# A hand-ordered attention and GeGLU kernel: the first norm of segments 2 and 3 is applied to x that the host has transposed

## The chip, the core and the metric

The kernel runs on one core of a Trainium2 chip. The metric is the device time of one execution in microseconds, as a median over runs. The engines are called as the profile calls them: PE is TensorE (matmul), DVE is VectorE, ACT is ScalarE, POOL is GpSimd, and SP is SyncE, which here only issues DMAs.

## The reference, cut to what matters

A pre-norm block with 2048 tokens of 512 channels. Its attention has 32 heads of 16 channels and four segments of 512 tokens; within a segment it is a masked softmax, and a memory carries what earlier segments held. A gated feed-forward block of width 1376 follows.

```python
x = A_x
h = x + _A_ref(_layernorm(x, axis=-1), A_wq, A_wk, A_wv, A_wo, A_beta)
h2 = h + _B_ref(_layernorm(h, axis=-1), B_w_gate, B_w_up, B_w_down)
```

The change touches only the first `_layernorm(x)`: for each token, (x - mean) / sqrt(variance + 1e-5) over the 512 channels.

## The kernel before

**Layout.** Rows of x have tokens on the partitions. The projections need the channels there, so each segment's normalized x is wanted transposed, as four tiles `XT[s][dc]` of 128 channels by 512 tokens. Every such tile is held as two parts, hi and lo: hi is the value rounded to the matmul's input type, lo the rest. A product is three matmuls (`SPLIT`: hi hi, hi lo, lo hi).

**The first norm.** `ln1_first` does segment 0 and `ln1(1)` segment 1; both take a square root on ACT and are not touched. `ln1(2)` and `ln1(3)` call `layer_norm` with `off=True`. Its steps for such a segment are: load four row tiles of x (L957); two sums per tile on ACT (L757, L766); small steps on DVE that work out 1/sqrt by Newton's method (`y`, four columns, one for each row tile) and `b = -mean * y` (L830); the scaling `y * x + b` on ACT, row tile by row tile (L834); the transposes on PE with the identity, 64 rows at a time (L847, by the helper `sides`, which also has DVE read one column between its two phases, L574); and `split_psum`, which copies a transposed bank to hi on ACT (L883) and subtracts for lo on DVE (L884).

**Attention.** The work is cut into 16 units of a group of 8 heads and a segment, in the order `UNITS`: segments 0 and 1 for all four groups, then segments 2 and 3. Each unit has two half units of four heads. A unit is projected (`project`, L978, and `vproj`, L1027, on 64-row tiles of PE); DMAs move queries and keys to the score layout (L1104, L1110); `pass_a` takes the score maxima (L1234 on PE, L1244 on DVE, L1258 and L1259 on POOL, L1265, and a store of the maxima into the query tile, L1272); `pass_b` makes scores (L1292), exponentials (L1298, ACT), a mask select on POOL (L1306), and the product with the values (L1320), which works on 32-column tiles of PE, as do the memory update (L1145) and the denominators (L1182).

**Feed-forward.** From about 390 us on, PE does nothing but the output projection and the feed-forward matmuls (L1393, L1584, L1651, L1752).

**The order.** Every instruction is first recorded with its engine and what it reads and writes. `ORDER`, a table of numbers, then says in which order they are issued: each engine works through its own part of that order, waiting on semaphores for what it needs. Buffers come from pools in that order too. The durations written in the code (`dve`, `act`, `pool`, `dma`) serve the search that made the table and decide which buffer is taken; they set no time on the chip. SP issues nearly all DMAs from one queue, also in order, so a DMA that waits holds back those behind it.

## Time and profile before

| what | value |
|---|---|
| median of 3 runs | 734.33 us (734.27 to 734.55) |
| the profiled execution | 732.46 us |
| its span, first to last instruction | 730.7 us |
| instructions | 19228 |
| granted TensorE clock, mean | 0.999 |
| busy: PE, DVE, ACT, POOL | 715.5, 630.8, 535.5, 521.7 us |

The profile is of one execution. A row of a group shows the line, the engine, the operation, what it writes and reads (buffer numbers left out), the count, the busy time in all, the mean of one in nanoseconds, and the idle time of the engine just before with what ended it. A row of the timeline shows the start, the length and the instructions merged into it. Ends of matmuls are modelled and overlap the next work, so starts are the better measure on PE.

### The profile page before, as it was taken

To read this page: it belongs to the slowest core of one execution; us is meant where nothing else is said; L and a number is where in the kernel's file an instruction comes from. 1 tells how busy PE (TensorE), PEld (TensorE's weight loads), DVE (VectorE), ACT (ScalarE), POOL (GpSimd) and SP (SyncE) were. 2 spreads that over 40 slices of the span, in tenths; PEclk is the share of its full clock that TensorE was granted. 3 is DMA by queue.
4 is the path that set the end of the run, shared out by engine and by line. 5 is a ranking of instruction groups with operands and counts; after the bars stand their busy time and mean duration, and the time that the engine had idled before them with its cause. 6 is when DMAs were issued, how large, how long until landed. Compare 5 with 4: busy or idle time off the path is not lost.

```text
span 730.7 us, 19228 instructions
## 1 busy us (share of the span) xinstructions
PE 715.5 (98%) x6436; PEld 573.9 (79%) x6436; DVE 630.8 (86%) x1998; ACT 535.5 (73%) x1139; POOL 521.7 (71%) x815
## 2 busy tenths in 40 slices
PE   6999999999999999999999999999999999999997
PEld 6887878777878887777677878888888878888885
DVE  6897889998979888999987576879999998879996
ACT  6889988797786887967868478678876766656431
POOL 7443434355553664878789999998999977699936
PEclk9999999999999999999999999999999999999999
DMA  7546457456577777687775756677574236876857
GB/s 274 147 119 161 109 125 217 116 133 190 160 182 185 206 201 210 193 232 218 190 229 185 224 159 220 218 204 240 162 201 129 81 105 212 250 241 226 272 132 260
DMA packets 100654, 137.32 MB, mean 188 GB/s; under 512 B 18012, under 2 KB 40460, under 8 KB 100556
## 3 DMA queue, kind: packets, MB, share of 16 engines
q1 hardware_dynamic: 100396, 135.84, 63.8%
q8 instruction: 51, 0.84, 0.5%
q14 instruction: 47, 0.39, 0.2%
q10 hardware_dynamic: 160, 0.26, 0.2%
HBM read 70.67 MB, written 39.26 MB: 150 GB/s over the span
## 4 chain that ended last, share of the span: by engine, by line
PE 89%; DVE 4%; DMA 2%; ACT 2%; POOL 1%; issue 1%; SPq 0%; DVEq 0%; ACTq 0%
PE bank L1584 29%; PE bank L1752 12%; PE bank L978 11%; PE bank L1320 10%; PE bank L1234 6%; PE bank L1292 6%; PE bank L1027 5%; PE bank L1393 3%; PE bank L1651 3%; PE bank L1400 2%; PE bank L1202 1%; POOL row L1306 1%; DVE bank L1244 1%; DMA stk<-slot 1%; DVE aside L1244 1%
## 5 line engine op out<-in xcount | busy, mean ns | idle before, releaser
L1298 ACT ACTIVATE row<-bank 128x512 f32<-128x512 f32 x320 | 171.7, 606 | 34.6 <-PE bank L1292 27.9
L1306 POOL TENSOR_SCALAR_AFFINE_SELECT row<-row 128x128 f32<-128x128 f32 (+1 forms) x320 | 107.1, 363 | 90.4 <-ACT row L1298 88.6
L1244 DVE CUSTOM_DVE_ANT_0 aside<-bank,amask 128x384 f32<-128x384 f32 (+2 forms) x384 | 141.3, 419 | 13.2 <-PE bank L1234 5.1
L978 PE MATMUL bank<-slot,slot 64*128 64x512 f32 x720 | 109.4, 402 | 0.0
L1584 PE MATMUL bank<-slot,slot 128*128 128x512 f32 (+1 forms) x366 | 95.7, 390 | 0.0
L1244 DVE CUSTOM_DVE_ANT_0 bank<-bank,amask 128x512 f32<-128x512 f32 x128 | 86.2, 712 | 9.0 <-PE bank L1234 7.8
L1292 PE MATMUL bank<-stq,stk 64*128 64x128 f32 (+3 forms) x512 | 81.2, 338 | 1.2 <-DVE slot L884 0.7
L1584 PEld LDWEIGHTS bank<-slot,slot 128*128 128x128 f32 (+1 forms) x366 | 67.6, 185 | 15.6
L1320 PE MATMUL bank<-row,vaug 128*32 128x512 f32 (+3 forms) x1024 | 77.1, 436 | 2.0 <-DVE nm L1244 0.8
L978 PEld LDWEIGHTS bank<-slot,slot 64*128 64x128 f32 x720 | 74.0, 185 | 6.4 <-DVE nm L1244 0.5
L1234 PE MATMUL bank<-stk,stq 64*128 64x128 f32 (+3 forms) x512 | 77.1, 327 | 1.2 <-DMA stk<-slot 0.8
L1763 DVE TENSOR_TENSOR row<-row,bank 128x512 f32<-128x512 f32 x110 | 71.9, 676 | 5.3 <-PE bank L1752 3.8
L1292 PEld LDWEIGHTS bank<-stq,stk 64*128 64x128 f32 x512 | 54.6, 185 | 13.9 <-DVE nm L1244 4.3
L1549 POOL TENSOR_TENSOR slot<-row,slot 128x512 fp32r<-128x512 f32 (+3 forms) x57 | 63.7, 1127 | 2.5 <-ACT slot L1547 2.2
L1591 ACT ACTIVATE vaug<-bank 128x512 f32<-128x512 f32 (+1 forms) x66 | 38.9, 595 | 34.4 <-PE bank L1584 33.8
L1234 PEld LDWEIGHTS bank<-stk,stq 64*128 64x128 f32 x512 | 53.4, 185 | 11.5 <-DVE nm L1244 3.0
L1320 PEld LDWEIGHTS bank<-row,vaug 128*32 128x32 f32 x1024 | 31.1, 109 | 38.3 <-issue 31.4
L1752 PE MATMUL bank<-slot,half 128*128 128x512 f32 x234 | 61.2, 389 | 0.0
L1027 PE MATMUL bank<-slot,slot 64*128 64x256 f32 x672 | 51.6, 284 | 0.3 <-DVE bn L763 0.2
L1752 PEld LDWEIGHTS bank<-slot,half 128*128 128x128 f32 x234 | 43.9, 188 | 9.2
L1244 DVE DVE_READ_ACCUMULATOR2_ANT nm<- 128x1 f32 x512 | 49.8, 97 | 0.0
L1027 PEld LDWEIGHTS bank<-slot,slot 64*128 64x128 f32 x672 | 47.4, 186 | 1.1 <-DVE bn L763 0.4
(230 smaller groups left out, 1715.6 us busy)
## 6 DMA issues: line engine op xcount, KB each, us to landing
stq<-slot SPq DMA_DIRECT2D x96, 128.0 KB
stk<-slot SPq DMA_DIRECT2D x94, 128.0 KB
row<-x SPq DMA_DIRECT2D x32, 256.0 KB
pv_dram<-row SPq DMA_DIRECT2D x32, 256.0 KB
row<-r_dram SPq DMA_DIRECT2D x28, 256.0 KB
wd_dram<-half SPq DMA_DIRECT2D x28, 256.0 KB
half<-wd_dram SPq DMA_DIRECT2D x28, 256.0 KB
row<-wg SPq DMA_DIRECT2D x20, 256.0 KB
```

The lines of the kernel that those rows point to most:

```text
L978: return nc.tensor.matmul(pm[i].t, w[i].t[rows_of(r), wi, dc * P:(dc + 1) * P], XT[s][dc].t[rows_of(r), xi, :], start=(dc, wi, xi, ph) == ...
L1027: return nc.tensor.matmul(pms[n].t[:, 256 * t:256 * t + 256], XT[s][dc].t[rows_of(r), xi, t0:t0 + P], whl[wi].t[rows_of(r), dc // 2, 256 * ...
L1234: nc.tensor.matmul(sa.t[:, c0:c0 + w], sq.t[own, p, i * P:(i + 1) * P], sk.t[own, p, 0:w], start=True, stop=True, tile_position=(64 * a, 0 ...
L1244: nc.vector.tensor_tensor_reduce(out=(sa.t[:, c0:c0 + w] if i > 2 else aside[:, turns[0]:turns[0] + w]), in0=sa.t[:, c0:c0 + w], in1=amask ...
L1292: nc.tensor.matmul(sc.t[:, c0:c0 + D - q0], sk.t[own, p, q0:q0 + P], sq.t[own, p, q0:D], start=True, stop=True, tile_position=(64 * a, 0), ...
L1298: act(w, prio, lambda sc=sc, e=e: nc.scalar.activation(e.t[:, :w], sc.t[:, :w], AF.Exp), [sc, vtab], [e])
L1306: nc.gpsimd.affine_select(v, v, pattern=pat + [[1, P]], compare_op=OP.is_ge, fill=0.0, base=0, channel_multiplier=-1)
L1320: nc.tensor.matmul(pv.t[32 * n:32 * n + 32, kb * P:D], va.t[:, 136 * kb + 17 * j:136 * kb + 17 * j + 32], e.t[:, lo:lo + D - kb * P], star ...
L1549: pool(0.14 + 2.13e-3 * (hi - lo), prio, lambda: nc.gpsimd.tensor_tensor(v.t[:, 1, :hi - lo], r.t[:, lo:hi], v.t[:, 0, :hi - lo].bitcast(F ...
L1584: nc.tensor.matmul(dst.t[:w], v.t[:, wi, c0 + j * w:c0 + (j + 1) * w], b[bk][j].t[:, xi, :], start=first and j == 0 and n == 0, stop=j == ...
L1752: nc.tensor.matmul(dst[u].t, ws[a].t[0][:, wi, P * u:P * u + P], h[bk].t[:, xi], start=first and m == 0, stop=m == 2, skip_group_check=True)
L1763: dve(D, prio, lambda u=u, acc=acc: nc.vector.tensor_tensor(acc.t, acc.t, src[u].t, op=OP.add), [src[u]], [acc])
```

## The change

For segments 2 and 3 the statistics stay as they were, on rows of x. What follows them is replaced by `across`. The host hands in a second copy of x, already transposed (`xt_in`). DVE copies `y` and `b` into one small tile, transposes that, and a DMA stores it to `n_dram` (16 KB); two DMAs then load from there the factors and the offsets along the tokens, each row repeated on all 128 partitions. For each of the four channel tiles a DMA loads x transposed, POOL multiplies and adds (two operations of 128x512), ACT copies to hi, and POOL subtracts for lo. Gone for the two segments are the scaling on ACT (L834), the transposes on PE (L847) with their DVE read (L574), the copies from PSUM (L883) and the subtraction on DVE (L884). DVE's Newton steps stay.

In counts over the whole program: L847 has 160 transposes before and 96 now; L884 20 and 12; L834 16 and 8; L883 20 and 12, with eight copies from SBUF in their place; POOL has 24 operations of 128x512 more, and one small memset; SP has 14 DMAs more (two stores, four loads of factors, eight of x transposed). ACT has one table load less. The table `ORDER` is new throughout, and the duration that it assumes for short DMAs is 0.7 for 0.65. Of its rows only the first is shown.

```diff
@@ -56,277 +56,277 @@
 ORDER = [
-    101, 0, 6, 10, 4, 5, 9, 11, 12, 92, 93, 94, 13, 14, 15, 17, 19, 2, 77, 95, 96, 97, 8, 29, 16, 18, 7, 28, 89, 90,
...
+    2, 6, 10, 5, 4, 11, 12, 8, 9, 13, 14, 29, 96, 93, 97, 7, 15, 16, 94, 95, 17, 18, 90, 91, 19, 99, 100, 28, 30, 92,
...
 ]
@@ -513,7 +513,7 @@
 @with_exitstack
 def infini_geglu(ctx: ExitStack, tc: tile.TileContext, x, wq, wk, wv, wo, beta,
-                 wg, wu, wd, wdp, out):
+                 wg, wu, wd, xt_in, wdp, out):
     nc = tc.nc
     p0 = ctx.enter_context(tc.tile_pool(name="p0", bufs=1))
     dram = ctx.enter_context(tc.tile_pool(name="dram", bufs=1, space=DRAM))
@@ -543,7 +543,7 @@
         return S.op("POOL", dur, prio, fn, ins, outs, **k)
     def dma(prio, fn, ins, outs, kb=256, dur=None, **k):
-        return S.op("SP", dur or (0.5 if kb == 256 else 0.65), prio, fn, ins, outs, lat=kb / 255, **k)
+        return S.op("SP", dur or (0.5 if kb == 256 else 0.7), prio, fn, ins, outs, lat=kb / 255, **k)
     def by_act(prio, fn, ins, outs):
         S.op("ACT", 0.45, prio, lambda: fn(nc.scalar), ins, outs, lat=2.4, chain=True)
@@ -620,11 +620,13 @@
     pv_dram = dram.tile([16, 2, P, D], F32, name="pv_dram")
     h_dram = dram.tile([T, D], F32, name="h_dram")
     t_dram = dram.tile([2, D, D], F32, name="t_dram")
+    n_dram = dram.tile([NSEG, 32, P], F32, name="n_dram")
+    yb = sb("yb", [P, 32])
     g_dram = dram.tile([T, D], F32, name="g_dram")
     y_dram = dram.tile([4, D, D], F32, name="y_dram")
     wd_dram = dram.tile([BY7[1], 7, P, 2, 256], F32, name="wd_dram")
-    vident, vamask, vmmask, vgt = (Val() for _ in range(4))
+    vident, vamask, vmmask, vgt, vyb = (Val() for _ in range(5))
@@ -733,7 +735,7 @@
                     tensor=to.tensor, offset=to.offset + k * P * D + a * P, ap=[[D, 32], [32 * D, 4], [1, P]]),
                     q.t[32 * a:32 * a + 32].rearrange("p (b x) -> p b x", b=4)), [q], [v], kb=70, dur=0.5, chain=True)
-    def layer_norm(prio, rows, dst, off=False, keep=None, acq=None, done=(), behind=(), scratch=None, by_side=False, swap=None):
+    def layer_norm(prio, rows, dst, off=False, keep=None, acq=None, done=(), behind=(), scratch=None, by_side=False, swap=None, seg=None):
         bn, mv = Val(PBN), Val(PMV)
         y = Val(PLN)
@@ -817,7 +819,7 @@
                 nc.vector.reciprocal(v_(), v_())
                 nc.vector.scalar_tensor_tensor(b.t, mv.t[:, :, 0], -1.0, v_(), op0=OP.mult, op1=OP.mult)
             dve(430, prio, inv, [v, mv], [y, b, v])
-            for t in range(4):
+            for t in range(4) if seg is None else []:
                 act(4, prio, lambda t=t: nc.scalar.activation(
                     rows[t].t, rows[t].t, AF.Identity, scale=y.t[:, t:t + 1], bias=b.t[:, t:t + 1]),
                     [b, y], [rows[t]], src=0.7)
@@ -829,6 +831,8 @@
             b = Val(PLN)
             dve(4, prio, lambda: nc.vector.scalar_tensor_tensor(
                 b.t, m_(), -1.0, y.t, op0=OP.mult, op1=OP.mult), [m, y], [b])
+        if seg is not None:
+            return across(prio, seg, y, b, dst)
         for t in [] if done else range(4):
             if off:
                 act(D, prio, lambda t=t: nc.scalar.activation(
@@ -876,6 +880,29 @@
             if dst[dc]:
                 split_psum(prio, pt, dst[dc])
+    def across(prio, s, y, b, dst):
+        vn, ab, zt = Val(), [Val(PROW), Val(PROW)], Val(PZ)
+
+        def pack():
+            nc.vector.tensor_copy(yb[:, 0:4], y.t)
+            nc.vector.tensor_copy(yb[:, 4:8], b.t)
+            nc.vector.transpose(zt.t, yb)
+        dve(400, prio, pack, [y, b, vyb], [zt, vyb])
+        dma(prio, lambda: nc.sync.dma_start(n_dram[s].rearrange("j (i q) -> i j q", i=4), zt.t), [zt], [vn], kb=16)
+        for i, r in enumerate(ab):
+            src = n_dram[s, 4 * i:4 * i + 4]
+            dma(prio, lambda src=src, r=r: nc.sync.dma_start(r.t, bass.AP(
+                tensor=src.tensor, offset=src.offset, ap=[[0, P], [1, D]])), [vn], [r])
+        for dc in range(ND):
+            r = Val(PROW)
+            dma(prio, lambda dc=dc, r=r: nc.sync.dma_start(r.t, xt_in[s * ND + dc]), [], [r])
+            for i, o in enumerate((OP.mult, OP.add)):
+                pool(1.24, prio, lambda i=i, o=o, r=r: nc.gpsimd.tensor_tensor(r.t, r.t, ab[i].t, op=o), [ab[i]], [r])
+            act(D, prio, lambda dc=dc, r=r: nc.scalar.activation(dst[dc].t[:, 0], r.t, AF.Copy), [r], [dst[dc]],
+                src=0.092)
+            pool(1.24, prio, lambda dc=dc, r=r: nc.gpsimd.tensor_tensor(
+                dst[dc].t[:, 1], r.t, dst[dc].t[:, 0].bitcast(F32), op=OP.subtract), [r], [dst[dc]])
+
     XL = [Val() for _ in range(ND)]
     XH, XLH = [[[Val() for _ in range(ND)] for _ in range(2)] for _ in range(2)]
@@ -957,7 +984,7 @@
             dma(prio - 3, lambda t=t, r0=r0: nc.sync.dma_start(rows[t].t, x[r0:r0 + P]), [],
                 [rows[t]])
         layer_norm(prio, rows, XT[s], off=s > 1, done=[Val()] if s < 2 else [],
-                   behind=[*XT[0], *XL] if s == 1 else [], scratch=PPV if s < 2 else PD, by_side=True)
+                   behind=[*XT[0], *XL] if s == 1 else [], scratch=PPV if s < 2 else PD, by_side=True, seg=s if s > 1 else None)
         if s < 2:
             pool(0.1, prio, lambda: nc.gpsimd.tensor_copy(tick, rows[3].t[:, 0:1]), [rows[3]],
@@ -1475,6 +1502,7 @@
     ln1_first()
+    pool(0.12, -3, lambda: nc.gpsimd.memset(yb, 0.0), [vcalm[0]], [vyb])
     ln1(1)
     act(1, -4.21 + DUE["l"][0], lambda: nc.scalar.activation(ones[:, 1:2], ones[:, 0:1], AF.Exp),
         [vtab, XT[0][3], *ROOTS], [vtab], src=1.4)
@@ -1883,6 +1911,8 @@
         "wg": ftiles(inputs["B_w_gate"]),
         "wu": ftiles(inputs["B_w_up"]),
         "wd": np.ascontiguousarray(np.asarray(inputs["B_w_down"])),
+        "xt": np.ascontiguousarray(np.asarray(inputs["A_x"]).reshape(NSEG, D, ND, P).transpose(0, 2, 3, 1).reshape(
+            NSEG * ND, P, D)),
         "wdp": np.ascontiguousarray(np.asarray(inputs["B_w_down"])[:2 * BY7[0] * P].reshape(-1, 4, 2, 2, 32).transpose(
             0, 3, 2, 1, 4).reshape(-1, D)),
     }
```

The three places that the prediction speaks of follow. Line numbers of the new kernel are higher than those of the kernel before: by 2 up to `layer_norm`, by 27 behind it, and by 28 from the call of `ln1(1)` on.

PE, before, where the last group of segment 2's transposes stands. `row` ahead is a row tile of x, `mb` and `vaug` belong to the memory update and the values.

```order
L1234 MATMUL bank_69<-stk_95,stq_100 128x512
L1145 MATMUL bank_68<-vaug_142,row_133 32x34 x16
L847 MATMUL bank_71<-ident,row_112 128x64
L847 MATMUL bank_72<-ident,row_112 128x64
L847 MATMUL bank_71<-ident,row_121 128x64
L847 MATMUL bank_72<-ident,row_121 128x64
L847 MATMUL bank_71<-ident,row_122 128x64
L847 MATMUL bank_72<-ident,row_122 128x64
L847 MATMUL bank_71<-ident,row_126 128x64
L847 MATMUL bank_72<-ident,row_126 128x64
L1320 MATMUL bank_70<-row_111,vaug_143 32x512
L1320 MATMUL bank_70<-row_113,vaug_143 32x512
```

And now, at the matching place of the order:

```order
L1261 MATMUL bank_69<-stk_91,stq_96 128x128
L1172 MATMUL bank_72<-vaug_144,row_131 32x34 x16
L1172 MATMUL bank_70<-vaug_142,row_121 32x34 x16
L1347 MATMUL bank_65<-row_129,vaug_143 32x512
L1347 MATMUL bank_65<-row_133,vaug_143 32x512
L1347 MATMUL bank_65<-row_104,vaug_143 32x512
L1347 MATMUL bank_65<-row_112,vaug_143 32x512
L1347 MATMUL bank_65<-row_135,vaug_143 32x384
L1347 MATMUL bank_65<-row_108,vaug_143 32x384
```

The memory update (L1145, now L1172) and the product with the values (L1320, now L1347) were parted by eight transposes; now two memory updates and the product stand together.

ACT, before, from the kernel's first instruction. L697 and L716 split weights, L919 is the square root of the first norm, L935 scales a row tile, L945 copies a transposed bank.

```order
L697 ACT_TABLE_LOAD
L697 ACTIVATE slot_73<-row_103 128x512
L919 ACT_TABLE_LOAD
L919 ACTIVATE bank_66<-bank_66 128x2
L935 ACTIVATE row_101<-row_101,ln_163,ln_162 128x512
L716 ACTIVATE slot_78<-row_106 128x512
L697 ACTIVATE slot_80<-row_109 128x512
L945 ACTIVATE slot_74<-bank_67 128x256
L919 ACTIVATE bank_66<-bank_66 128x2
L945 ACTIVATE slot_75<-bank_68 128x256
```

And now:

```order
L946 ACT_TABLE_LOAD
L946 ACTIVATE bank_66<-bank_66 128x2
L718 ACTIVATE slot_73<-row_106 128x512
L699 ACTIVATE slot_74<-row_107 128x512
L962 ACTIVATE row_103<-row_103,ln_163,ln_162 128x512
L699 ACTIVATE slot_79<-row_109 128x512
L718 ACTIVATE slot_73<-row_110 128x512
L946 ACTIVATE bank_66<-bank_66 128x2
L972 ACTIVATE slot_75<-bank_67 128x256
L972 ACTIVATE slot_77<-bank_69 128x256
```

The first of the two table loads is gone, the square root stands first, two weight splits stand ahead of the scaling (L962) and two ahead of the second root and the copies (L972).

SP, before, in the middle of the attention stage, where factors are stored to `r_dram` (L1195, L1356) and loaded again (L1214):

```order
L1195 DMA r_dram<-z_138 4x32x32
L1356 DMA r_dram<-cd_136 16x8x32
L1348 DMA cd_137<-pv_dram 128x1x32
L1342 DMA pv_dram<-row_109 128x512
L1214 DMA row_132<-r_dram 128x1x512
L1214 DMA row_102<-r_dram 128x1x512
L1356 DMA r_dram<-cd_137 16x8x32
L1110 DMA stk_94<-slot_77 32x2x512
L1110 DMA stk_95<-slot_81 32x2x512
L1272 DMA stq_97<-mx_157 4x8x128
```

And now, at segment 3's store of the factors (L891) and the first load of them (L894):

```order
L891 DMA n_dram<-z_139 4x32x32
L1241 DMA row_133<-r_dram 128x1x512
L1299 DMA stq_96<-mx_157 4x8x128
L698 DMA row_108<-wq 128x512
L894 DMA row_134<-n_dram 128x512
L1390 DMA o_dram<-row_101 128x4x128
L1131 DMA stq_99<-slot_75 32x2x512
L898 DMA row_111<-xt 128x512
L1369 DMA pv_dram<-row_102 128x512
L1131 DMA stq_99<-slot_75 32x2x512
L894 DMA row_114<-n_dram 128x512
```

The pair through `n_dram` is new; three DMAs stand between its store and its first load. Behind that load stand a store of the outputs and moves of queries (L1131).

540 rows, old and new, of the table ORDER are left out of this document.

## Prediction

> **What bounds the kernel now.** I read the page first (busy shares and the chain that ended last), then the busy time by stage, then the waits of TensorE.
>
> ```profile
> PE 715.5 (98%) x6436; PEld 573.9 (79%) x6436; DVE 630.8 (86%) x1998; ACT 535.5 (73%) x1139; POOL 521.7 (71%) x815
> PE 89%; DVE 4%; DMA 2%; ACT 2%; POOL 1%; issue 1%; SPq 0%; DVEq 0%; ACTq 0%
> ```
>
> TensorE is busy for 98% of the span and makes 89% of the chain. The second view cuts the span into the start, the attention stage, the feed-forward stage and the tail. Its columns are the length, then the busy time of PE, PEld, DVE, ACT and POOL.
>
> ```profile
> 0.00:24.50 24.50, 18.33 (x126) 16.61 (x126) 15.69 (x52) 17.36 (x41) 17.50 (x38) 1.00 0.74 240
> 24.50:390.00 365.50, 361.21 (x4833) 282.45 (x4834) 324.75 (x1379) 297.21 (x662) 208.68 (x474) 1.00 0.65 178
> 390.00:726.00 336.00, 335.98 (x1478) 274.87 (x1476) 289.56 (x567) 220.91 (x439) 295.53 (x304) 1.00 0.63 194
> 726.00:730.70 4.70, 0.00 (x0) 0.00 (x0) 0.77 (x2) 0.00 (x0) 0.00 (x0) 0.81 0.70 264
> ```
>
> From 390 to 726 us TensorE has no gap, and the change leaves its work there alone. The tail is stores. So the time can change only in the first 390 us. There TensorE idles for 6.17 us at the start and for 4.29 us in 365.5 us of attention. VectorE is at 324.75 of 365.5 there (89%), ScalarE at 81%, GpSimd at 57%: the change takes work from the first three and gives it to the fourth.
>
> ```profile
> PE bank L913 <- DMA row<-x: 4.3, 1, 4.3
> PE bank L940 <- ACT row L935: 1.2, 1, 1.2
> PE bank L1234 <- DMA stk<-slot: 0.8, 1, 0.8
> PE bank L1320 <- POOL row L1306: 0.5, 1, 0.5
> ```
>
> TensorE's waits are total, number, longest. Apart from the first load none is over 1.2 us. There is no big stall to win; what can go is TensorE's own time.
>
> **The 64 transposes (shorter).** Segments 2 and 3 have eight groups of eight L847 transposes. The busy time of L847 in their two windows, and the first and the last group with the instruction that follows each:
>
> ```profile
> 115.00:131.00 16.00, 1.95 (x32) 1.00 0.67 181
> 160.00:170.00 10.00, 1.97 (x32) 1.00 0.66 183
> 115.22 0.41 PE L847 MATMUL bank<-ident,row 64*128 64x64 f32 x8
> 115.57 0.33 PE L1145 MATMUL bank<-vaug,row 128*32 128x34 f32 x15
> 169.30 0.47 PE L847 MATMUL bank<-ident,row 64*128 64x64 f32 x8
> 169.55 0.49 PE L978 MATMUL bank<-slot,slot 64*128 64x512 f32 x1
> ```
>
> From a group's first start to the next work's start it is 0.35 us for the first and 0.25 for the last; the eight of them, measured so, make 2.8 us. Busy time says 3.92, but its ends overlap the next work. I take **-2.8 us**. The Trainium skill (Trainium Kernel Development and Optimization, Performance Expectations) says that matmul busy time misleads because matmuls are pipelined; by busy time the sum below would end 1.1 us lower.
>
> **Fewer changes of tiling (shorter).** L1320, L1145 and L1182 work on 128*32 tiles, nearly all else in this stage on 64*128. Counted over TensorE's whole order, uninterrupted stretches of these three lines are 43 before and 34 now; the order pieces ahead show one place. What a stretch costs beyond its work is read from one stretch of 32 and one of 64 (end of a stretch), and from the same four L1234 instructions ahead of a stretch and ahead of other 64-row work (its beginning):
>
> ```profile
> 231.82 2.36 PE L1320 MATMUL bank<-row,vaug 128*32 128x512 f32 x32
> 234.11 0.50 PE L1234 MATMUL bank<-stk,stq 64*128 64x512 f32 x2
> 384.30 4.51 PE L1320 MATMUL bank<-row,vaug 128*32 128x512 f32 x64 [0.24 <-POOL stk L1549]
> 388.75 0.73 PE L1584 MATMUL bank<-slot,stq 128*128 128x512 f32 x2
> 210.98 0.48 PE L1234 MATMUL bank<-stk,stq 64*128 64x384 f32 x4
> 211.39 0.42 PE L1320 MATMUL bank<-row,vaug 128*32 128x256 f32 x4
> 27.29 0.45 PE L1234 MATMUL bank<-stk,stq 64*128 64x384 f32 x4
> 27.54 0.28 PE L847 MATMUL bank<-ident,row 64*128 64x64 f32 x2
> ```
>
> Two stretches of 32 take 2 x 2.29 = 4.58 us, one of 64 takes 4.45: 0.13 for one more end. Ahead of a stretch the four take 0.41, else 0.25: up to 0.16 for a beginning, but other causes may be in that. So a stretch costs 0.13 to 0.29; I take 0.22, as both rows show a cost, and 9 x 0.22 = **-2.0 us** (-1.2 to -2.6). The skill's page TensorEngine Tiling (Array Packing), Key Properties, says that changing the tiling mode drains TensorE. By it both sides cost in full, and the term would be 2.6.
>
> **The start (shorter).** The first norm is kept, but its steps stand in another order: one table load on ScalarE is gone, and the loads of x come ahead of the weights.
>
> ```profile
> 5.17 0.63 ACT L697 ACTIVATE slot<-row 128x512 fp32r<-128x512 f32 x1 [3.08 <-DMA row<-wk]
> 5.81 1.28 ACT L919 ACT_TABLE_LOAD   x1
> 7.77 0.81 ACT L935 ACTIVATE row<-row,ln,ln 128x512 f32<-128x512 f32 x1 [0.51 <-DVE ln L926]
> 10.00 0.38 ACT L945 ACTIVATE slot<-bank 128x256 fp32r<-128x256 f32 x1 [0.38 <-PE bank L940]
> 10.71 0.16 ACT L919 ACTIVATE bank<-bank 128x2 f32<-128x2 f32 x1 [0.32 <-DVE bank L917]
> 3.54 0.69 DVE L908 BATCH_NORM_STATS2 bn<-row 128x6 f32<-128x512 f32 x1 [3.54 <-DMA row<-x]
> 10.44 2.20 PE L999 MATMUL bank<-slot,slot 128*128 128x256 f32 x10
> 12.48 1.03 PE L940 MATMUL bank<-ident,row 128*128 128x128 f32 x8
> 24.59 0.73 PE L1234 MATMUL bank<-stk,stq 64*128 64x256 f32 x8 [0.77 <-DMA stk<-slot]
> ```
>
> The first load is there at 3.54, the third at 5.17: 0.82 us each, so by this the fourth comes at 6.0, the fifth at 6.8, the eighth at 9.3. Without the table load at 5.81 the first root (L919) can run over a microsecond earlier. But ScalarE now has the splits of loads four and five (0.63 each) ahead of L935: 6.8 + 0.63 = 7.45, then 0.81 gives 8.3, against 8.6 before. The copies after the first transposes (L945) wait behind the split of load eight and the second root: 9.3 + 0.63 + 0.16 = 10.1, against 10.0. So TensorE's first projections start as before, at 10.44. The second root itself comes at 9.9 instead of 10.71, 0.8 earlier, and with it the transposes of 12.48 and what follows them without a gap. I take **-0.8 us**, bounds -1.1 and +0.3 (if a weight lands late).
>
> **What is added, and its cover.** The rows are the split that leaves VectorE and the scaling that leaves ScalarE, and then, for 40 to 240 us alone, the GpSimd operations nearest to the new ones and the mask selects.
>
> ```profile
> L884 DVE TENSOR_TENSOR slot<-bank,slot 128x512 fp32r<-128x512 f32 x20 | 13.0, 680 | 1.4 <-ACT slot L883 1.4
> L834 ACT ACTIVATE row<-row,ln,ln 128x512 f32<-128x512 f32 x16 | 12.9, 818 | 1.1 <-DVE ln L830 1.1
> L702 POOL TENSOR_TENSOR slot<-row,slot 128x512 fp32r<-128x512 f32 x10 | 12.9, 1292 | 2.2 <-ACT slot L697 1.3 <-ACT mx L1269 0.9
> L1359 POOL TENSOR_TENSOR row<-row,row 128x512 f32<-128x512 f32 x6 | 7.7, 1286 | 0.0
> L1306 POOL TENSOR_SCALAR_AFFINE_SELECT row<-row 128x256 f32<-128x256 f32 (+1 forms) x168 | 56.1, 362 | 64.7 <-ACT row L1298 63.4 <-PE bank L978 0.3 <-POOL row L1306 0.2
> ```
>
> VectorE loses eight subtractions, 8 x 0.68 = 5.4 us, and gets six small steps of the packing; ScalarE loses eight scalings, 8 x 0.82 = 6.5 us, and its eight copies stay (now from SBUF: 0.63, L697 above). GpSimd gets 24 operations of 1.29 us, 31 us. They fit: GpSimd idles for 64.7 us ahead of the selects alone. All of it I set at nothing for the sum. The new chain has time: in GpSimd's order the last step of segment 2 stands after the selects of 8 half units, while TensorE first reads segment 2 after 11 of 32 half units are finished; for segment 3 it is 13 and 16. A half unit is about 365 / 32 = 11 us, so some 30 us of cover each.
>
> SP gets 14 more DMAs. One loads what another stored, and SP waits in order, so what stands behind waits too.
>
> ```profile
> SPq L1214 <- DMA r_dram<-cd: 5.7, 2, 3.4
> 83.71 0.59 SPq L1110 DMA_DIRECT2D stk<-slot  x1
> ```
>
> The existing pair of that kind waited 5.7 us in two places, 3.4 at most. Segment 2 has eight DMAs between store and load, segment 3 only three, 3 x 0.59 = 1.8 us. Behind it stand two stq moves for the scores and a store. Cost on the path: 0 to 3.4; I take **+0.5**, since TensorE waited only 0.8 us for such moves in all.
>
> Sum: -2.8 - 2.0 - 0.8 + 0.5 = -5.1 us. The profiled execution took 732.46 us, its span 730.7 and 1.8 around it; it would become 727.4. The median of the runs is 734.33, 1.9 above, and becomes **729.2 us**.
>
> **The rivals.** *Slower: GpSimd holds the selects.* All 24 new operations stand among selects, and L1320 needs the selects. Four selects each held for a whole operation (4 x 1.29 = 5.2 us) eat the gain; from six on (6 x 1.29 = 7.7) it is slower by over 0.2%; at ten (12.9), 742 us. The skill's GPSIMD Engine Reference, Key points, speaks for this: elementwise work is about twice as fast on VectorE, and the trace agrees (1286 to 680 ns). Against it: 16 operations of that length in the two rows above already stood among the selects of 40 to 240 us, and TensorE waited for a select once, 0.5 us. Chance 0.08.
>
> *Nearly the same: SP holds the moves.* The wait for the stored factors is as long as the longest of its kind, 3.4, and falls on TensorE: -5.6 + 3.4 = -2.2, and with the low price of a stretch -1.4: 732.1 to 732.9 us. For it: only three DMAs in between. Against it: the cover of the moves before. Chance 0.14.
>
> *More: waits go too.* VectorE, the fullest of the others, gets 5 us lighter, and half of the 4.29 us of attention idle goes: -5.1 - 2.1 = -7.2, 727.1 us, with the high price of a stretch 726.5. For it: the waits on VectorE and on moves. Against it: they are short and spread. Chance 0.14.
>
> That the transposes stay is excluded: L847 has 160 instructions in the order before, 96 now.
>
> **How the numbers follow.** The forecast has 0.64. Its own bounds are -2.8 - 1.2 + 0.3 + 0.5 = -3.2 and -2.8 - 2.6 - 1.1 = -6.5. The range reaches to the rivals of nearly the same and of more, with 0.7 us more idle gone on the low side: 725.8 to 733.0. A run of this kernel can tell about 0.2%, 1.5 us. Faster by more than that: the forecast, the third rival, and a good part of the second, 0.82. Within it: the rest of the second, and places where both rivals act a little, 0.10. Slower: the first, 0.08.
>
> **What would show it.** In the new profile the transposes (L847 by the old numbers) should have 96 records, the first score product after the start (L1234) should come at about 23.8 us, the stage without gaps on TensorE should begin some 5 us earlier and be as long, and TensorE's wait for mask selects should stay under 2 us. I am wrong if those waits add up to several us, if SP's wait for the stored factors ends late ahead of a move that TensorE waits for, or if the saved transposes come back as short idle times of the same sum.

## The result and the profile after

The changed kernel takes 728.19 us (median of 6 runs, 727.14 to 729.08), the kernel before 734.44 (6 runs, 732.09 to 735.11): ratio 0.9918, 95% interval 0.9901 to 0.9934. The prediction was 729.2, 1.0 more. A second set on another occasion gave 727.93 against 733.90, ratio 0.9923 (0.9902 to 0.9945). The profiled execution took 727.89 us, its span is 726.2, 4.5 less than before.

The page of the changed kernel, busy time by engine and the chain that ended last:

```profile
PE 710.5 (98%) x6372; PEld 572.7 (79%) x6372; DVE 627.3 (86%) x1992; ACT 528.7 (73%) x1130; POOL 551.6 (76%) x840
PE 65%; POOL 3%; DVE 3%; DMA 1%; issue 1%; SPq 1%; ACT 0%; POOLq 0%; ACTq 0%
```

TensorE has 64 instructions fewer, GpSimd 29.9 us more (31 foreseen), ScalarE 6.8 us less (6.5 foreseen), VectorE only 3.5 less (5.4 foreseen, before the packing). The busy time by stage has the columns length, PE, PEld, DVE, ACT, POOL:

```profile
24.50:390.00 365.50, 361.50 (x4794) 286.42 (x4793) 324.61 (x1378) 296.48 (x659) 246.44 (x507) 1.00 0.69 188
390.00:726.00 336.00, 330.74 (x1454) 270.24 (x1452) 286.82 (x563) 215.30 (x429) 290.91 (x299) 1.00 0.63 195
```

TensorE idles 4.00 us in the first row, 4.29 before. That row now holds 6.8 us of the feed-forward stage; cut at the ends of the attention stage itself (24.59 to 388.75, and 24.30 to 383.24) TensorE idles 4.20 us before and 4.00 after, while GpSimd's busy time goes from 207.43 to 240.43 us. The waits hardly changed, so the gain must lie in TensorE's own time. The timeline of TensorE gives the ends of the stages, first in the changed kernel, then for the last work of the kernel before (its other ends stand in the prediction: 24.59 and 388.75):

```profile
24.30 1.03 PE L1261 MATMUL bank<-stk,stq 64*128 64x256 f32 x12 [1.22 <-DMA stq<-slot]
378.80 4.51 PE L1347 MATMUL bank<-row,vaug 128*32 128x512 f32 x64 [0.28 <-POOL row L1333]
383.24 1.66 PE L1612 MATMUL bank<-slot,slot 128*128 128x512 f32 x6
718.54 2.20 PE L1679 MATMUL bank<-slot,stq 128*128 128x512 f32 x9
```

```profile
724.46 1.52 PE L1651 MATMUL bank<-slot,stk 128*128 128x512 f32 x6
```

So the 4.5 us of the span divide like this (us):

```
                                          before            after             difference
start, to the first score product         24.59             24.30             -0.29
attention, to the work behind L1320/1347  388.75 - 24.59    383.24 - 24.30    -5.22
from there to TensorE's last              725.98 - 388.75   720.74 - 383.24   +0.27
tail                                      730.7 - 725.98    726.2 - 720.74    +0.74
```

What the attention stage wins, 5.22, is as much as the whole forecast; the start gave less than foreseen, and the tail took 0.7 back. There the last addition of VectorE now waits for a GpSimd addition:

```profile
721.33 0.69 DVE L1683 TENSOR_TENSOR row<-row,bank 128x512 f32<-128x512 f32 x1 [0.48 <-POOL row L1818]
```

TensorE's waits after (total, number, longest):

```profile
PE bank L1261 <- DMA stq<-slot: 1.2, 1, 1.2
...
PE bank L1347 <- POOL row L1333: 0.3, 1, 0.3
```

The mask selects cost TensorE 0.3 us. Nothing shows here that GpSimd is near a limit. The experiments show it.

### The profile page after: what moved, and what is told of

Read it like the earlier page. It is cut to its first block, busy times and chain, and to the rows that moved or that the text cites. A ratio compares the mean times of both kernels' runs of the same rounds, so it can differ in the third digit from the quotient of the medians.

```text
span 726.2 us, 19132 instructions
## 1 busy us (share of the span) xinstructions
PE 710.5 (98%) x6372; PEld 572.7 (79%) x6372; DVE 627.3 (86%) x1992; ACT 528.7 (73%) x1130; POOL 551.6 (76%) x840
## 4 chain that ended last, share of the span: by engine, by line
PE 65%; POOL 3%; DVE 3%; DMA 1%; issue 1%; SPq 1%; ACT 0%; POOLq 0%; ACTq 0%
PE bank L1612 27%; PE bank L1780 12%; PE bank L1005 5%; PE bank L1347 5%; PE bank L1420 3%; PE bank L1261 3%; PE bank L1319 3%; PE bank L1054 2%; PE bank L1427 2%; PE bank L1679 2%; POOL row L1333 1%; DVE aside L1271 1%; PE bank L1229 1%; DVE bank L1271 1%; DMA row<-y_dram 1%
## 5 line engine op out<-in xcount | busy, mean ns | idle before, releaser
L1333 POOL TENSOR_SCALAR_AFFINE_SELECT row<-row 128x256 f32<-128x256 f32 (+1 forms) x320 | 107.8, 364 | 69.4 <-ACT row L1325 68.7
L1271 DVE CUSTOM_DVE_ANT_0 aside<-bank,amask 128x256 f32<-128x256 f32 (+2 forms) x384 | 140.1, 419 | 12.3 <-PE bank L1261 6.8
L1005 PE MATMUL bank<-slot,slot 64*128 64x512 f32 x720 | 109.4, 400 | 0.0
L1612 PE MATMUL bank<-slot,slot 128*128 128x512 f32 (+1 forms) x348 | 90.9, 391 | 0.0
L1319 PE MATMUL bank<-stq,stk 64*128 64x512 f32 (+3 forms) x512 | 80.6, 335 | 0.1
L1261 PE MATMUL bank<-stk,stq 64*128 64x128 f32 (+3 forms) x512 | 78.6, 328 | 2.0 <-DMA stq<-slot 1.2
L1005 PEld LDWEIGHTS bank<-slot,slot 64*128 64x128 f32 x720 | 76.2, 185 | 4.3 <-ACT row L1366 0.2
L1347 PE MATMUL bank<-row,vaug 128*32 128x512 f32 (+3 forms) x1024 | 75.9, 435 | 1.2 <-DVE nm L1271 0.5
L1612 PEld LDWEIGHTS bank<-slot,slot 128*128 128x128 f32 (+1 forms) x348 | 64.6, 186 | 15.0 <-issue 0.4
L1261 PEld LDWEIGHTS bank<-stk,stq 64*128 64x128 f32 x512 | 55.3, 185 | 11.3 <-issue 2.5
L1780 PE MATMUL bank<-slot,half 128*128 128x512 f32 x240 | 64.0, 390 | 0.0
L1319 PEld LDWEIGHTS bank<-stq,stk 64*128 64x128 f32 x512 | 54.4, 185 | 12.1 <-DVE nm L1271 2.6
L1619 ACT ACTIVATE vaug<-bank 128x512 f32<-128x512 f32 (+1 forms) x66 | 38.6, 592 | 31.2 <-PE bank L1612 31.1
L1347 PEld LDWEIGHTS bank<-row,vaug 128*32 128x32 f32 x1024 | 31.6, 109 | 35.1 <-issue 29.7
L1054 PE MATMUL bank<-slot,slot 64*128 64x256 f32 x672 | 51.3, 283 | 0.3 <-DVE row L1040 0.3
L1054 PEld LDWEIGHTS bank<-slot,slot 64*128 64x128 f32 x672 | 47.0, 186 | 1.4 <-DVE row L1040 0.5
```

Of the source, the lines that this page charges most:

```text
L1005: return nc.tensor.matmul(pm[i].t, w[i].t[rows_of(r), wi, dc * P:(dc + 1) * P], XT[s][dc].t[rows_of(r), xi, :], start=(dc, wi, xi, ph) == ...
L1054: return nc.tensor.matmul(pms[n].t[:, 256 * t:256 * t + 256], XT[s][dc].t[rows_of(r), xi, t0:t0 + P], whl[wi].t[rows_of(r), dc // 2, 256 * ...
L1261: nc.tensor.matmul(sa.t[:, c0:c0 + w], sq.t[own, p, i * P:(i + 1) * P], sk.t[own, p, 0:w], start=True, stop=True, tile_position=(64 * a, 0 ...
L1271: nc.vector.tensor_tensor_reduce(out=(sa.t[:, c0:c0 + w] if i > 2 else aside[:, turns[0]:turns[0] + w]), in0=sa.t[:, c0:c0 + w], in1=amask ...
L1319: nc.tensor.matmul(sc.t[:, c0:c0 + D - q0], sk.t[own, p, q0:q0 + P], sq.t[own, p, q0:D], start=True, stop=True, tile_position=(64 * a, 0), ...
L1333: nc.gpsimd.affine_select(v, v, pattern=pat + [[1, P]], compare_op=OP.is_ge, fill=0.0, base=0, channel_multiplier=-1)
```

## The experiments

The start differs by up to 3.3 us from trace to trace (last section but one), so beside the runs I compare the attention stage: from the first score product to the start of the work behind the last L1347, by the same two rows of each trace.

```
kernel                          median us  ratio to before (95%)     stage us
before                          -          1                         364.16
changed                         728.19     0.9918 (0.9901-0.9934)    358.94
changed, again                  727.93     0.9923 (0.9902-0.9945)    358.19
before, no transposes           735.60     1.0018 (1.0005-1.0030)    365.23
before, transposes twice        733.38     0.9992 (0.9980-1.0005)    363.55
changed, transposes back        729.56     0.9950 (0.9932-0.9967)    360.83
changed, stretches split        732.29     0.9970 (0.9958-0.9982)    362.19
changed, in the old order       736.78     1.0040 (1.0022-1.0057)    366.62
changed, GpSimd's work twice    756.85     1.0313 (1.0297-1.0330)    386.06
changed, 8 GpSimd operations +  736.13     1.0027 (1.0009-1.0045)    366.96
changed, less GpSimd            729.31     0.9930 (0.9906-0.9955)    358.86
changed, loads moved at start   731.25     0.9962 (0.9945-0.9979)    363.07
changed, a move by ScalarE      729.25     0.9934 (0.9912-0.9955)    358.71
changed, warm start             728.45     0.9935 (0.9918-0.9953)    358.63
```

Five traces of kernels that leave this stage as the changed one has it, or only take work from it (changed twice, less GpSimd, a move by ScalarE, warm start), lie at 358.2 to 358.9, mean 358.67: the stage is known to about 0.4 us. The stage before is known from one trace.

**The transposes in the old order.** The theory was that they cost TensorE's own time; the rival, that they fill time in which it would wait.

```
-            sides(pts, [[step(t) for t in range(4)]],
+            sides(pts, [[step(t) for t in range(4)] * times],   # segments 2, 3: times = 0, or 2
```

> The kernel before, with its own order, but the 64 transposes of segments 2 and 3 are left out (the copies and subtractions behind them read whatever the banks hold, so the result is not the reference's). Everything else stays: VectorE, ScalarE and GpSimd have the work of before. Theory (a transpose costs what lies from start to start, 2.8 us for the 64): 2.8 us less than before, ratio 0.996. Rival A (busy time counts, 3.9 us): ratio 0.9947. Rival B (the transposes only fill time in which TensorE would wait for others): under 0.7 us less, ratio over 0.999.

> The kernel before, with its own order, but each of the 64 transposes of segments 2 and 3 is made twice, back to back in its group (same result). Theory (start to start): another 32 ns each within a group, so 2.0 us more, up to 2.8 if the end of a group counts again; ratio 1.0027 to 1.0038. Rival A (busy time, 3.9): 1.0053. Rival B (they only fill waiting time): under 0.7 us more, ratio under 1.001.

Without them the kernel is 0.18% slower, with twice as many it is not slower (0.9992, interval across 1). The theory fell for the old order. That it is even slower fits a lower clock: the mean granted clock is 0.9960 over its 12 runs and 0.9979 over the 29 runs of the kernel before, and 0.0019 of 734 us is 1.4 us, as much as the medians differ (1.3). Three pieces of TensorE's timeline at one place show why: before, without, and twice.

```profile
129.12 0.46 PE L847 MATMUL bank<-ident,row 64*128 64x64 f32 x8
129.51 2.36 PE L1320 MATMUL bank<-row,vaug 128*32 128x512 f32 x32
132.56 0.50 PE L1292 MATMUL bank<-stq,stk 64*128 64x256 f32 x4 [0.69 <-DVE slot L884]
```

```profile
26.59 0.73 PE L1234 MATMUL bank<-stk,stq 64*128 64x256 f32 x8 [0.72 <-DMA stk<-slot]
130.44 2.36 PE L1320 MATMUL bank<-row,vaug 128*32 128x512 f32 x32 [0.22 <-DVE tock L574]
134.19 0.50 PE L1292 MATMUL bank<-stq,stk 64*128 64x256 f32 x4 [1.40 <-DMA stq<-mx]
```

```profile
24.93 0.74 PE L1234 MATMUL bank<-stk,stq 64*128 64x256 f32 x8 [0.83 <-DMA stk<-slot]
129.78 0.54 PE L847 MATMUL bank<-ident,row 64*128 64x64 f32 x12
132.54 0.50 PE L1292 MATMUL bank<-stq,stk 64*128 64x256 f32 x4
```

The second product of this half unit (L1292) comes 108.0, 107.6 and 107.6 us after the first score product, with 32 transposes of segment 2 ahead of it, with none and with 64. It needs the row maxima, which travel scores, maxima, turn, mx, a DMA into stq; without the transposes TensorE is there early and waits 1.40 us for that DMA. Before, it waited 0.69 (put down to a VectorE subtraction), with twice as many transposes not at all. Later in the same trace the granted clock fell as well (columns as in the stages above; behind the busy times stand the clock, the DMA share and GB/s):

```profile
160.00:170.00 10.00, 9.28 (x92) 4.55 (x84) 7.31 (x26) 8.01 (x19) 2.90 (x9) 0.83 0.54 148
```

10 x 0.17 = 1.7 us lost. Why the clock fell just there is not settled. So in the old order the saved time of segment 2 came back as waiting, as the wait of 1.40 us shows, the very thing that the prediction named as its third way to be wrong.

**The transposes in the new order.** Dummies put them back, without the work of the other engines.

```
             def go(i, r, ph):
+                for k in range(4) if more and (dc, wi, xi, ph) == (0, 0, 0, 0) else []:
+                    nc.tensor.transpose(pm[i].t[:, k * 64:k * 64 + 64], ident[rows_of(r), :], ...)
                 return nc.tensor.matmul(
```

> The changed kernel with its own order, but TensorE makes 64 more transposes of 64 columns again: eight (of the identity, into banks that the projection overwrites) at the head of each of eight projections of segments 2 and 3. The work of the other engines stays as in the changed kernel, the result too. Theory now (where nothing else binds, a transpose costs TensorE's own time): 64 x 28 ns = 1.8 us by what one takes in the middle of a group, up to 2.8 by the predicted price, more than the changed kernel of the same call. Rival (transposes fill time in which TensorE would wait, in either order): under 0.7 us more.

> The changed kernel itself once more, as the measure for the runs of this call: 728 us, ratio 0.992 to before.

The stage of the kernel with the dummies (its lines from L1005 on are 7 higher):

```profile
24.66 1.02 PE L1268 MATMUL bank<-stk,stq 64*128 64x256 f32 x12 [1.16 <-DMA stq<-slot]
385.49 1.65 PE L1619 MATMUL bank<-slot,slot 128*128 128x512 f32 x6
```

360.83 is 2.2 us over the mean of 358.67, the medians differ by 1.6, the ratios by 0.0027, 2.0 us. The intervals of the two ratios overlap; the stage, whose five traces differ by 0.8 at most, is the better evidence, and TensorE's idle time in it is no larger (3.6 us). So here a transpose costs 25 to 34 ns of TensorE, close to the 26 to 35 from one start to the next within the six groups of before that nothing interrupts: the new order has no wait at these places that would swallow it. The same 64 transposes are worth nothing in one order and 2 us in the other.

**The stretches.** Fifteen entries of the order were moved; TensorE's instructions stay the same.

```
 c: L1347 x32 | L1347 x32 | r: L1261 x4 ...      34 stretches of 128*32
 c: L1347 x32 | r: L1261 x4 | c: L1347 x32 ...   49
```

> The changed kernel with 15 entries of its order moved: in 15 stretches of 128*32 work one 64-row step that stood behind the stretch now stands inside it, so TensorE has 49 such stretches instead of 34 and the same instructions. Theory (0.22 us for each further stretch): 3.3 us more than the changed kernel, about 731.5 us (0.13 each: 2.0 more; 0.29 each: 4.4 more). Rival (a stretch costs nothing of its own; what the new order won there was short waits): under 0.7 us more, or as much more as TensorE's listed waits grow.

```profile
26.60 1.04 PE L1261 MATMUL bank<-stk,stq 64*128 64x256 f32 x12 [1.15 <-DMA stq<-slot]
388.79 1.65 PE L1612 MATMUL bank<-slot,slot 128*128 128x512 f32 x6
```

362.19 less 358.67 is 3.5 us, 0.23 each; by the ratios 0.0047 to 0.0052, 3.5 to 3.8 us. TensorE's listed waits did not grow to match. The rival fell: a stretch costs 0.23 to 0.25 us of its own, and the nine that went are worth 2.1. The rule of the Trainium skill (TensorEngine Tiling (Array Packing), Key Properties) that a change of tiling mode drains TensorE gives no price; that each further stretch cost time here agrees with it.

**The order.** All old operations in their old places, the new ones fitted in (the removed by their lines before, the new by theirs after, counted in instructions).

```
 ORDER = [   # of before, renumbered
-    L834 x4, L847 x32, L574 x2, L883 x4, L884 x4 of segment 2, and of segment 3
+    L886, L891, L894 x2, L898 x4, L900 x8, L901 x4, L903 x4 of each
```

> The changed kernel's operations in the order of before: all the old operations keep their places, and only the new ones (packing, store, loads, 24 GpSimd operations, eight copies) are put in where buffers and inputs allow, spread over GpSimd's selects. 42 stretches of 128*32 work. Theory (the new norm alone gains little; the gain needs the order that was searched with it): with the transposes gone the waits of the old order come back, and GpSimd's new operations hold selects, so no gain: 733 us or more. Rival (the norm alone brings the predicted 2.8 us, the order the rest): 731 to 732 us.

It is 2.9 us slower than before. Its waits:

```profile
PE bank L1319 <- DMA stq<-mx: 4.5, 3, 1.8
```

It is the wait of the experiment without transposes, three times over: the maxima's move is late ahead of L1319 (L1292 before). The new operations' places here were mine, so this is not the best that the old order allows; it shows that the operations alone, put at these places, bring no gain.

**GpSimd's reserve.**

```
-            pool(1.24, prio, lambda ...: nc.gpsimd.tensor_tensor(... subtract), [r], [dst[dc]])
+            ... the subtraction twice (8 more); twice and two more with each addition (24 more);
+            or 64 of its 512 columns (less)
```

> The changed kernel with 24 more GpSimd operations of 128x512: each multiplication is followed by addition, subtraction and addition of the second factor instead of one addition, and each subtraction of the low half is made twice (same result but for rounding). 24 x 1.29 = 31 us more of GpSimd in the same places of its order. Theory (the operations lie in GpSimd's idle time): within 0.7 us of the changed kernel, 728 to 729 us, and TensorE's wait for mask selects under 2 us. Rival (GpSimd holds the selects): 1.29 us for every operation that holds one; with half of the 24 held 15 us more, 743 us.

> The changed kernel with 8 more GpSimd operations of 128x512 only: each subtraction of the low half is made twice (same result). 8 x 1.29 = 10.3 us more. With 24 more (31 us) 27 us of it reached the end. Theory A (GpSimd's reserve is used up by the 24 operations of the change, everything further is on the path): about 8 to 10 us more than the changed kernel. Theory B (there is a reserve of several operations for each segment; only the long chains of the doubled version broke it): under 2 us more.

> The changed kernel with GpSimd's eight subtractions of the low half cut to 64 of 512 columns (the rest of the low half keeps what the buffer held, so the result is not the reference's); some 9 us less of GpSimd. With 8 subtractions more 8 us of 10.3 reached the end. Theory A (the order just fits: nothing waits for these operations now, so less of them brings nothing): within 0.7 us of the changed kernel, and TensorE's waits as before. Theory B (GpSimd already binds here): several us less, up to 8, about 720 to 725 us.

24 operations more cost 28.8 us of 31 by the medians, 8 more cost 8.2 of 10.3, and 8 shortened ones win nothing. My theory of idle time that covers them fell. The end of segment 2 in the changed kernel, on GpSimd, and TensorE's first use of that segment:

```profile
128.97 1.29 POOL L903 TENSOR_TENSOR slot<-row,slot 128x512 fp32r<-128x512 f32 x1
130.20 0.20 POOL L1285 CAST mm<-nm 128x16 fp32r<-128x16 f32 x1
```

```profile
129.95 0.87 PE L1054 MATMUL bank<-slot,slot 64*128 64x256 f32 x12
130.65 0.39 PE L1319 MATMUL bank<-stq,stk 64*128 64x512 f32 x2
130.88 0.88 PE L1054 MATMUL bank<-slot,slot 64*128 64x256 f32 x12
```

And in the kernel with 8 more, where two L903 stand for one:

```profile
133.17 2.63 POOL L903 TENSOR_TENSOR slot<-row,slot 128x512 fp32r<-128x512 f32 x2
```

```profile
133.27 0.77 PE L1054 MATMUL bank<-slot,slot 64*128 64x256 f32 x10
135.85 0.48 PE L1054 MATMUL bank<-slot,slot 64*128 64x256 f32 x2 [1.81 <-POOL slot L903]
...
186.48 0.78 PE L1347 MATMUL bank<-row,vaug 128*32 128x256 f32 x5 [1.68 <-POOL row L1333]
```

The wait falls on the last two of the second group of L1054. In the changed kernel these start at about 131.5, and the L903 that they need ends at 130.3: the step had 1.2 us of cover. Where GpSimd is late it holds the first projections of the segment, then the selects behind it. With 24 more the maxima too, which two small GpSimd operations prepare (L1285 and L1286; all lines from L905 on are 5 higher there):

```profile
PE bank L1297 <- POOL mm L1291: 6.8, 4, 2.8
PE bank L1352 <- POOL row L1338: 6.5, 3, 4.2
...
PE bank L1059 <- POOL slot L908: 1.8, 1, 1.8
```

These waits are not the whole cost. TensorE's idle time in the stage is 8.5 us with 8 more and 19.5 with 24 more (4.0 in the changed kernel), and the granted clock fell behind some of the waits: in the trace with 8 more to 0.50 from 136.0 to 139.4 us, behind the wait of 1.81 above (1.7 us lost), in the one with 24 more to 0.50 for 20.5 us of the stage, 10.2 us lost:

```profile
26.34:412.40 386.06, 366.57 (x4764) 287.10 (x4764) 320.18 (x1369) 291.24 (x648) 270.30 (x523) 0.97 0.62 173
```

Its four runs have mean clocks of 0.983 to 0.989, against 0.996 to 1.000 in the changed kernel. So about a third of the 28.8 us is a lower clock, and not waiting.

**The start.** The last value projection of the start, before and in the changed kernel:

```profile
17.90 5.92 PE L1039 MATMUL bank<-slot,slot 128*128 128x256 f32 x48
```

```profile
10.02 1.48 PE L1026 MATMUL bank<-slot,slot 128*128 128x256 f32 x10 [0.65 <-ACT slot L972]
11.34 1.42 PE L967 MATMUL bank<-ident,row 128*128 128x128 f32 x8
17.17 5.92 PE L1066 MATMUL bank<-slot,slot 128*128 128x256 f32 x48
```

It ends 0.73 us earlier. How much of this is the new order is not shown: the first ten projections take 1.32 us from start to start here, and 2.04 in the kernel before (10.44 to 12.48, rows in the prediction), as that trace was at half rate up to 12.1 us (see the section on the hardware). But the first score product then waits 1.22 us for a stq move instead of 0.77 for a stk move. Two attempts at that wait:

```
 SP's order:  stq x3 | xt | x | stq | wq ... stq x2        (changed)
 SP's order:  stq x4 | wq ... stq x2 | x | xt              (loads moved)
-    third stq move of half unit 0 on SP's queue
+    the same on ScalarE's queue                           (a move by ScalarE)
```

> The changed kernel with two entries of SP's order moved: the load of the first transposed tile of segment 2 and a load of x, which stood ahead of the fourth stq move at 21.5 and 22.2 us, stand behind the last stq moves of the first unit. Theory (these loads share the DMA engines with the three stq moves that the first score product needs): the first score product's wait of 1.2 us shrinks by 0.5 us or more, the first score product comes up to a microsecond earlier, about 727.5 us. Rival (they were issued after the last needed move, at 20.6 us, and cost nothing; that move's own issue and flight set the time): wait 1.1 to 1.2 us as before, 728 us.

> The changed kernel, but the last of the moves that the first score product needs (the third stq move of half unit 0) is issued by ScalarE's queue, behind the two moves there, instead of as the fourth in SP's row. Theory (four moves of 0.7 to 0.8 us each in a row on SP set the first score product's start): its wait falls from 1.2 to about 0.5 us, and the time by 0.7 us, to 727.4 us. Rival (the flight of the moves, 2.9 us after the last issue, is bound by the DMA engines): nothing is gained.

Neither edit won anything: the wait stayed at 1.45 and 1.34 us. The first theory fell. The second was not tested, since ScalarE issued the move at 23.77 us, 2.45 behind the first of these moves (21.32), while SP had issued it 2.03 behind (20.32 and 18.29). The first edit even cost 4.4 us of the stage, since the load of x that moved belongs to segment 1, whose statistics were then late:

```profile
35.22 0.69 PE L851 MATMUL bank<-ident,row 64*128 64x64 f32 x8 [1.68 <-DVE bn L765]
```

```profile
24.50:60.00 35.50, 31.96 (x351) 26.34 (x351) 29.03 (x136) 25.74 (x61) 15.38 (x34) 0.90 0.54 148
```

By the second view, 35.5 x 0.10 = 3.5 us are a lower clock. So a DMA that costs nothing in SP's row is not free to move. What sets the flight of the last move stays open.

> The changed kernel with two small edits: three transposes of the identity (into columns of a bank that are not used then, 0.2 us each) at the head of the first projection, where TensorE waits for the first split columns; and one load of y_dram near the end moved ahead of a store to the output in SP's order. Theory: in the profiles so far, where TensorE idled 1.7 us or more in all between 7 and 12 us, its granted clock was 0.50 for 3.4 us afterwards and 1.7 us were lost (five of six traces with 1.7 us or more), and nothing was lost below that; the fillers take 0.6 us of idle away, so the clock stays at 1.00, runs in which it dropped (about a third for the changed kernel) lose 1.7 us no more, and the last GpSimd additions end up to 0.4 us earlier: 0.5 to 1 us less than the changed kernel, 727.2 us. Rival (the drop has another cause, or the fillers hold up the first projection): 728 us or more, with the clock at 0.50 for 3.4 us in the start of some runs as before.

```
+                        for n in range(3) if (cols.start, dc, ks) == (0, 0, ((0, 0), (1, 0))) else []:
+                            nc.tensor.transpose(pm[0].t[:, 256:384], ident, ident)
```

Besides, one load of `y_dram` near the end stands ahead of a store in SP's order. In its profile the gaps between 7 and 12 us are gone, the first score product comes at 24.12 and the span is 724.3, the shortest of all. Its 6 runs, 726.03 to 730.33, are not faster than those of the changed kernel (0.9935 against 0.9918 and 0.9923, intervals that overlap): not shown to be better. One of the six has a mean clock of 0.996, as have the traces of changed again and of split stretches, whose clock dropped.

## Why the prediction was right, step by step

**Transposes, -2.8: about -2.1, and not by itself.** Put back in the new order they cost 1.6 to 2.2 us. The step took start to start of whole groups, with the change of work at each end; what is saved is nearer to 64 times the spacing inside a group. What the step did not say is that it holds only where no wait stands behind. In the old order it is worth nothing. The prediction's fear, "the saved transposes come back as short idle times of the same sum", came true in the kernel with the old order, and the newly searched order is what avoids it.

**Stretches, 9 x 0.22 = -2.0: right.** Fifteen more cost 0.23 to 0.25 each.

**Start, -0.8: -0.3.** The step that failed is "with it the transposes of 12.48 and what follows them without a gap": TensorE's own chain did come 0.73 earlier, but the first score product waits for moves, which came only 0.3 earlier. The step also took the times of before as those of the order alone, though that trace ran at half rate up to 12.1 us; what the order is worth at an equal clock stays open. (Its 6.8 + 0.63 is 7.43, not 7.45; nothing hangs on that.)

**SP's hold, +0.5: 0.** In SP's row the store of segment 3 and the load behind it, with three DMAs between as foreseen:

```profile
140.58 0.56 SPq L891 DMA_DIRECT2D n_dram<-z  x1
...
142.88 0.44 SPq L698 DMA_DIRECT2D row<-wq  x1
143.42 0.37 SPq L894 DMA_DIRECT2D row<-n_dram  x1
```

The load follows 0.1 us behind the DMA ahead of it: the stored factors were there.

**GpSimd at nothing: right value, wrong reason.** The step "The new chain has time", with its "some 30 us of cover each", failed. It counted half units in GpSimd's order against half units that TensorE had finished; but GpSimd's selects run ahead of the products that use them, and this lead ate the difference. The cover was 1.2 us for segment 2; for segment 3 it was not measured. The slow rival set its turning point at six held selects and gave it 0.08; with eight operations more in the same places the change would have been slower than before (1.0027). What kept it on the right side is that the order was searched with these operations in it: less GpSimd work wins nothing, more costs nearly all of itself, in waits and in lost clock. That the term came out at nothing was luck as far as the prediction's reason goes.

**The rest.** Of the stage's 5.5 us (364.16 to the mean of 358.67) transposes and stretches explain 4.2 to 4.3. Some 0.3 us are idle time, about 1 us stays without a shown cause. It made up for the start and for the 1.0 us given back behind the attention stage, which the prediction had not looked at. So the two main terms are right in kind and nearly in size, but that the sum came within 1.0 us is in part luck: errors of 0.5 to 1 us each cancel.

## What the runs showed of the hardware

TensorE's rate at the start differs between executions, of the same kernel too. In every trace its first matmuls, from 4.3 us on, start 0.213 us apart; later, with the clock at 1.00, 128x128 transposes of this kind start 0.109 apart. So it begins at half rate. The kernel before stayed there up to 12.1 us: 15 matmuls in 3.41 us, then 30. (The clock column says 1.00 in both rows; the first clock record of this trace is at 12.10, and a stretch without a record is printed as 1.00. There only the count tells.)

```profile
8.69:12.10 3.41, 3.41 (x15) 3.18 (x16) 3.34 (x11) 2.71 (x8) 3.00 (x3) 1.00 1.05 403
12.10:15.50 3.40, 3.40 (x30) 3.40 (x30) 2.28 (x9) 3.40 (x10) 2.28 (x7) 1.00 1.04 383
```

The clock changes only every 3.41 us, at places that differ from trace to trace. In six traces it rose between 9.1 and 12.5 us and stayed up. In six others it rose at 7.1 to 8.1, and fell to 0.50 one step of 3.41 us later, for one step. In two, the old order and the move by ScalarE, it rose only at 15.4 and 16.4. From 11.5 to 15 us, in the changed kernel, in the one with split stretches and in the one with a move by ScalarE:

```profile
11.50:15.00 3.50, 3.50 (x29) 3.18 (x28) 3.36 (x13) 3.42 (x13) 3.50 (x10) 1.00 1.05 393
```

```profile
11.50:15.00 3.50, 3.50 (x19) 3.50 (x19) 2.80 (x8) 2.33 (x6) 3.23 (x12) 0.53 1.06 399
```

```profile
11.50:15.00 3.50, 3.50 (x19) 3.50 (x18) 2.61 (x7) 2.15 (x6) 3.22 (x12) 1.00 1.05 398
```

The first score product came at 24.1 to 24.9 us in the first six, at 25.8 to 26.6 in the six with the drop, at 26.5 and 27.5 in the last two, and for the same kernel at 24.30 and 25.80: this is why the stage, and not the whole span, is compared above. What decides shows when the traces are cut into steps of 3.41 us, counted from the first clock record. Here the changed kernel, again, at its rise and its drop, and the kernel with 8 more at the longest idle time that brought no drop:

```profile
7.09:10.50 3.41, 1.70 (x11) 0.97 (x10) 2.74 (x10) 3.31 (x9) 1.74 (x2) 1.00 1.02 381
10.50:13.92 3.42, 3.42 (x17) 3.42 (x18) 2.93 (x8) 2.46 (x7) 3.14 (x12) 0.50 1.06 398
```

```profile
183.78:187.19 3.41, 1.73 (x32) 0.86 (x27) 2.79 (x11) 0.81 (x2) 3.33 (x5) 1.00 0.82 223
```

In the first, TensorE idled 1.71 us in gaps of 0.39, 0.37 and 0.95. Over all 14 traces, some 2900 steps, every step at full clock with 1.71 us or more of idle time, half of the step, was followed by one at 0.50: 11 of 11. Of the others, with up to 1.68 us, two were: without transposes at 161.7 us (0.45 us idle) and with loads moved at 31.1 (1.26); their cause stays open. A step at 0.50 was followed by full clock where TensorE idled 0.38 us or less in it, and not where it idled 0.70 to 0.92 (three steps). The Trainium skill (TensorE: Matmul & The Clock Gate, Part 1, What's actually happening) puts half rate behind an idle window of some 3.4 us. The length agrees; the condition doesn't: here idle time of half that length was enough, in gaps of 0.95 us and less.

## What to carry to other kernels

An instruction taken from the busiest engine is worth its time only if no other chain arrives at the next meeting point at the same moment: leave it out in the old order, and see whether the time moves, before the rest of the change is built around it. Cover has to be read in microseconds between the end of the one step and the start of its reader, not in units of two orders counted from different points; where it can't be read, adding a few operations of the same kind in the same place measures it at once. Short waits close together can cost more than their length, since the clock may fall behind them: read the granted clock of each run beside its time. Where an order is searched anew with a change, the gain belongs to both together, and neither has a price of its own.
